# Moving two loads ahead of two transposing DMAs in a fused state-space and feed-forward kernel

## The chip, the cores and the metric

The kernel runs on one core of a Trainium2 chip. The metric is the device time of one execution in microseconds; the span of a profile (first to last instruction) is some 1.8 us shorter. Engines are named as in the profile: PE is TensorE, PEld its weight loads, DVE VectorE, ACT ScalarE, POOL GpSimd, SPq the queue on which SyncE issues DMAs. "L845" is a line of the kernel.

## The reference, cut to what matters

```python
xn  = layernorm(x)                                   # x: 2048 x 512, bf16
out = x + A(xn) + B(xn)
B   = (silu(xn @ w_gate) * (xn @ w_up)) @ w_down     # 512 -> 1376 -> 512
# A: a complex diagonal recurrence over the 2048 rows
#    u = B_bar xn;  h[t] = Lam_bar * h[t-1] + u[t];  y = 2 Re(C h) + xn * Dskip
```

## The kernel before

The 2048 rows are worked on in four chunks of 512. A chunk is loaded (`x_sb`), normalised (`xn_sb`), transposed by a DMA (`xnT`; chunk 2's is laid into `scrC`), multiplied with the gate and up weights and with B, scanned on VectorE, and projected down with `wd` and the C weights `W`, which are made from the transposed C matrices (`CT`, laid into `hss`).

Every operation is a task with its dependencies; a list scheduler then orders the tasks of ScalarE, VectorE and GpSimd by their estimated times. The orders of TensorE and of the DMA queue are those of the program. Two rules matter here. A transposing DMA waits for all DMAs before it, and DMAs after it wait for it:

```python
if xpose:
    after = after + tuple(dma_tasks)
    fn = lambda e, dst=dst, src=src: e.dma_start_transpose(out=dst, in_=src)
...
else:
    if xp_state[0] is not None:
        after = after + (xp_state[0],)
```

And `xn_sb` holds twelve 128-row tiles for sixteen, so chunk 3 is normalised into the place of chunk 0, after chunk 0's skip product (which needs `dsk`, the skip vector) and the sum that follows it (`resid_chunk`). The program, in the part concerned:

```python
xt_chunk_dma(1)          # transpose of chunk 1
loads_stage_b2()         # x of chunk 2, C matrices, skip vector, x of chunk 3
...
xt_chunk_dma(2)
dma("ld_wd0", wd[:, 0:FT - 1, :], ...)      # down weights, 1280 KB
dma("ld_wd1", wd[0:fsz[-1], FT - 1, :], ...)
...                      # gate, up of chunk 1; B of chunk 2
resid_chunk(0)
ln_chunk(3)
xt_chunk_dma(3)
ffn_left()               # leftover gate and up columns of all four chunks (L845, L855)
dc_chunk(0)              # first down projection (L966, L977, L980)
```

Of the kernel before, what the change touches and what calls it, by code (L numbers as in the profile page):

```python
# [249 lines left out]
def bass_parallel_sum__ssm_conv_s5__swiglu_ffn__prompt_kernel(  # L250
# [32 lines left out]
    with es:  # L283
        block = es.enter_context(nc.Block(no_gpsimd_drain=True))

        def sb(name, shape, dt):
            return es.enter_context(nc.sbuf_tensor(name, shape, dt))
# [7 lines left out]
        x_sb = sb("x_sb", [128, NT, D], B16)  # L295
# [14 lines left out]
        dsk = sb("dsk", [128, D], B16)  # L310
# [77 lines left out]
        x_v = A_x[0].rearrange("(a p) d -> p a d", p=128)  # L388
# [7 lines left out]
        def dma(name, dst, src, writes, nbytes, reads=(), after=(), out_=False, eng="sp", xpose=False, prio=0.0, order=(), **kw):  # L396
            after = tuple(after)
# [3 lines that stand above are left out]
                est, nb = 1900.0, int(nbytes * 1.2) + 140000  # L401
# [3 lines that stand above are left out]
                fn = lambda e, dst=dst, src=src: e.dma_start(dst, src, **kw)  # L405
                est, nb = 330.0 + nbytes / 900.0, nbytes
            t = g.add(eng, fn, reads=reads, writes=writes, name=name, dma=True, after=after, out=out_, est=est, nbytes=nb, prio=prio, order=order)
            dma_tasks.append(t)
            if xpose:
                xp_state[0] = t  # L410
            return t

        TILEB = 128 * D * 2
# [33 lines left out]

        def loads_stage_b2():
            dma("ld_x8", x_sb[:, 8:12, :], x_v[:, 8:12, :], [("x", a) for a in range(8, 12)], 4 * TILEB)
            dma("ld_cre", CT[:, 0], A_C_re, [("CT", 0)], 512 * 512 * 2, xpose=True)  # L450
            dma("ld_cim", CT[:, 1], A_C_im, [("CT", 1)], 512 * 512 * 2, xpose=True)
            dma("ld_dsk", dsk[:], A_Dskip.partition_broadcast(128), [("dsk",)], 128 * 1024)
            dma("ld_x12", x_sb[:, 12:16, :], x_v[:, 12:16, :], [("x", a) for a in range(12, 16)], 4 * TILEB)

        g.add("pool", lambda e: e.memset(epst[:], EPS), writes=[("epst",)], name="epst", est=100)
        g.add("pool", lambda e: e.memset(mhalf[:], -0.5), writes=[("mhalf",)], name="mhalf", est=100)
# [541 lines left out]
        loads_stage_b1()  # L998
        xt_chunk_dma(1)
        loads_stage_b2()  # L1000
        for ip in range(0, 3):
            ffn_up(0, ip)
# [97 lines left out]
```

## Time and profile before

| | before |
|---|---|
| time, median of 3 runs | 178.94 us (178.79 to 179.15) |
| the profiled execution | 179.2 us, span 177.4 us |
| TensorE, VectorE, ScalarE busy | 98%, 92%, 49% |
| TensorE waiting for data after 13.59 us | 0.33 us, at 64.52 |

The DMA queue in order of time shows the line of waits. Columns: start, time of the issue alone, queue and line, kind, destination and source.

```profile
42.16 0.34 SPq L405 DMA_DIRECT2D dsk<-in_A_Dskip_dram  x1
42.54 0.44 SPq L405 DMA_DIRECT2D x_sb<-in_A_x_dram  x1
47.35 1.69 SPq L400 DMA_TRANSPOSE scrC<-xn_sb  x1
51.62 1.14 SPq L405 DMA_DIRECT2D wd<-in_B_w_down_dram  x2
60.56 1.99 SPq L400 DMA_TRANSPOSE xnT<-xn_sb  x1
```

The short issue times are not the transfers; how long a transfer holds the queue is read from the distance to the next line. The skip vector and x of chunk 3 hold the queue from 42.16 to 47.35 us; the down weights hold it for 8.9 us, and only then does the transpose of chunk 3 go out. The rest of the profile before is read in the prediction.

### The profile page before, as it was taken

To read this page: it belongs to the slowest core of one execution; us is meant where nothing else is said; L and a number is where in the kernel's file an instruction comes from. 1 tells how busy PE (TensorE), PEld (TensorE's weight loads), DVE (VectorE), ACT (ScalarE), POOL (GpSimd) and SP (SyncE) were. 2 spreads that over 40 slices of the span, in tenths; PEclk is the share of its full clock that TensorE was granted. 3 is DMA by queue.
4 is the path that set the end of the run, shared out by engine and by line. 5 is a ranking of instruction groups with operands and counts; after the bars stand their busy time and mean duration, and the time that the engine had idled before them with its cause. 6 is when DMAs were issued, how large, how long until landed. Compare 5 with 4: busy or idle time off the path is not lost.

```text
span 177.4 us, 2425 instructions
## 1 busy us (share of the span) xinstructions
PE 173.9 (98%) x935; PEld 83.8 (47%) x935; DVE 162.5 (92%) x283; ACT 86.9 (49%) x116; POOL 11.1 (6%) x22
## 2 busy tenths in 40 slices
PE   8999999999999999999999999999999999999994
PEld 2894444444444434444444444444444444444644
DVE  2964999899899999999999999999999999999943
ACT  4679889979978869240456554000265520000000
POOL 3040500050050000000000000000000000000000
PEclk9999999999999999999999999999999999999999
DMA  5992595563468150001100000001100000000032
GB/s 169 268 373 68 120 148 95 161 133 82 134 133 283 29 102 0 0 4 66 54 0 0 0 0 4 0 0 59 59 0 4 0 0 0 0 0 30 32 110 67
DMA packets 22966, 12.37 MB, mean 70 GB/s; under 512 B 15180, under 2 KB 22956, under 8 KB 22956
## 3 DMA queue, kind: packets, MB, share of 16 engines
q1 hardware_dynamic: 22652, 11.77, 24.9%
q10 hardware_dynamic: 304, 0.46, 0.8%
q8 instruction: 7, 0.11, 0.3%
q14 instruction: 3, 0.02, 0.0%
HBM read 6.46 MB, written 2.10 MB: 48 GB/s over the span
## 4 chain that ended last, share of the span: by engine, by line
PE 62%; DMA 19%; DVE 7%; ACT 4%; SPq 3%; POOL 1%; issue 1%; ACTq 0%
PE pb L966 20%; PE pb L762 19%; PE pb L980 16%; DMA x_sb<-in_A_x_dram 7%; DMA xnT<-xn_sb 5%; PE pb L883 4%; SPq L405 3%; DVE st L483 3%; DMA hss<-in_A_C_im_dram 3%; DMA hss<-in_A_C_re_dram 2%; DMA dsk<-in_A_Dskip_dram 2%; PE pb L977 2%; ACT xn_sb L507 2%; DVE hT L834 1%; PE pb L855 1%
## 5 line engine op out<-in xcount | busy, mean ns | idle before, releaser
L923 DVE TENSOR_TENSOR_SCAN rot<-sm,car,rot 128x512 bf16<-128x512 f32 x32 | 38.8, 1266 | 0.0
L774 ACT ACTIVATE sg<-pb 128x1024 bf16<-128x1024 f32 x20 | 20.1, 1023 | 32.1 <-PE pb L762 31.3
L966 PE MATMUL pb<-wd,hT 128*128 128x512 bf16 (+2 forms) x180 | 35.2, 355 | 0.0
L980 PE MATMUL pb<-W,hss 128*128 128x512 bf16 (+2 forms) x144 | 30.3, 355 | 0.0
L762 PE MATMUL pb<-xnT,wu 128*128 128x512 bf16 x120 | 27.9, 379 | 0.0
L966 PEld LDWEIGHTS pb<-wd,hT 128*128 128x128 bf16 x180 | 16.8, 98 | 18.2 <-ACT scrC L730 0.4
L832 ACT ACTIVATE uf<-pb 128x1024 bf16<-128x1024 f32 x20 | 20.5, 1024 | 8.9 <-PE pb L762 7.3
L762 PE MATMUL pb<-xnT,wg 128*128 128x512 bf16 x92 | 21.8, 379 | 0.0
L883 PE MATMUL pb<-xnT,BT 128*128 128x512 bf16 x96 | 21.0, 379 | 0.0
L980 PEld LDWEIGHTS pb<-W,hss 128*128 128x128 bf16 x144 | 13.5, 97 | 14.4
L762 PEld LDWEIGHTS pb<-xnT,wu 128*128 128x128 bf16 x120 | 11.7, 98 | 14.2 <-ACT sg L774 0.2
L890 ACT ACTIVATE u_sb<-pb 128x1024 bf16<-128x1024 f32 x16 | 16.0, 1022 | 3.3 <-PE pb L883 3.3
L883 PEld LDWEIGHTS pb<-xnT,BT 128*128 128x128 bf16 x96 | 9.3, 98 | 11.4 <-DMA BT<-in_A_B_im_dram 0.3
L985 DVE TENSOR_TENSOR x_sb<-pb,x_sb 128x512 bf16<-128x512 f32 (+2 forms) x18 | 11.1, 628 | 3.3 <-PE pb L980 3.0
L762 PEld LDWEIGHTS pb<-xnT,wg 128*128 128x128 bf16 x92 | 9.0, 98 | 10.6
L834 DVE TENSOR_TENSOR hT<-sg,uf 128x1024 bf16<-128x1024 bf16 x20 | 13.4, 681 | 0.4 <-ACT uf L832 0.4
L483 DVE BATCH_NORM_STATS2 st<-x_sb 128x6 f32<-128x512 bf16 x12 | 7.4, 679 | 3.1 <-DMA x_sb<-in_A_x_dram 3.1
L914 DVE TENSOR_TENSOR rot<-u_sb,cosT 128x2048 bf16<-128x2048 bf16 x8 | 9.7, 1218 | 0.0
L914 DVE TENSOR_TENSOR rot<-rot,sin 128x2048 bf16<-128x2048 bf16 x8 | 9.7, 1218 | 0.0
L914 DVE TENSOR_TENSOR rot<-u_sb,sin 128x2048 bf16<-128x2048 bf16 x8 | 9.7, 1218 | 0.0
L914 DVE TENSOR_TENSOR rot<-rot,cosT 128x2048 bf16<-128x2048 bf16 x8 | 9.7, 1213 | 0.0
L914 DVE TENSOR_TENSOR rot<-rot 128x2048 bf16<-128x2048 bf16 x8 | 9.6, 1218 | 0.0
(93 smaller groups left out, 180.4 us busy)
## 6 DMA issues: line engine op xcount, KB each, us to landing
out_dram<-x_sb SPq DMA_DIRECT2D x15, 128.0 KB, 1.7
x_sb<-in_A_x_dram SPq DMA_DIRECT2D x3, 512.0 KB, 4.7
wd<-in_B_w_down_dram SPq DMA_DIRECT2D x1, 1280.0 KB, 8.6
wu<-in_B_w_up_dram SPq DMA_DIRECT2D x1, 768.0 KB, 5.0
wu<-in_B_w_up_dram SPq DMA_DIRECT2D x1, 608.0 KB, 7.0
x_sb<-in_A_x_dram SPq DMA_DIRECT2D x4, 128.0 KB, 3.2
wg<-in_B_w_gate_dram SPq DMA_DIRECT2D x1, 480.0 KB, 5.9
wg<-in_B_w_gate_dram ACTq DMA_DIRECT2D x1, 448.0 KB, 3.8
```

Source lines behind the costliest of these rows:

```text
L483: return g.add("dve", lambda e, a=a: e.bn_stats(out=st[:, a % 8, :], in_=x_sb[:, a, :]), reads=[("x", a)], writes=[("st", a % 8), ("st0", ...
L762: inst = e.matmul(pbank[0:fs, bk, :].rearrange("p (j t) -> p j t", j=4), lhsT=w[:, kt, i * 128:i * 128 + fs], rhs=xnT[c][:, :, kt, :], sta ...
L774: g.add("act", lambda e: e.activation(out=sg[rows, sl, 0:n, :].rearrange("p a t -> p (a t)"), in_=pair_f32(rows, bk, 512 * n), func=AF.Sil ...
L832: g.add("act", lambda e: e.activation(out=uf[rows, ul, 0:n, :].rearrange("p a t -> p (a t)"), in_=pair_f32(rows, bk, 512 * n), func=AF.Ide ...
L834: g.add("dve", lambda e: e.tensor_tensor(out=hT[rows, hb, i0:i0 + n, :], in0=sg[rows, sl, 0:n, :], in1=uf[rows, ul, 0:n, :], op=ALU.mult), ...
L883: inst = e.matmul(pbank[:, bk, :].rearrange("p (j t) -> p j t", j=4), lhsT=BT[:, ri, kt, pt * 128:(pt + 1) * 128], rhs=xnT[c][:, :, kt, :] ...
L890: g.add("act", lambda e: e.activation(out=u_sb[:, us].rearrange("p r t -> p (r t)"), in_=pair_f32(slice(0, 128), b0), func=AF.Identity), r ...
L914: tt = lambda out, a, b, op, r, w, nm: g.add("dve", lambda e: e.tensor_tensor(out=out, in0=a, in1=b, op=op), reads=r, writes=w, name="%s_% ...
L923: g.add("dve", lambda e, A0=A0, A1=A1, k=k, ri=ri, pt=pt: e.tensor_tensor_scan(out=A1[:, k, ri, :], data0=rr[:, pt:pt + 1].to_broadcast([1 ...
L966: inst = e.matmul(pbank[:, bk, 0:nc_], lhsT=hT[0:fs, hb, i, lt * 128:(lt + 1) * 128], rhs=wd[0:fs, i, c0:c0 + nc_], start=(i == 0), stop=F ...
L980: inst = e.matmul(pbank[:, bk, 0:nc_], lhsT=hss[:, hb, pt, ri, lt * 128:(lt + 1) * 128], rhs=W12[:, ri, pt, c0:c0 + nc_], start=False, sto ...
L985: g.add("dve", lambda e, bk=bk, a=a, c0=c0, nc_=nc_: e.tensor_tensor(out=x_sb[:, a, c0:c0 + nc_], in0=pbank[:, bk, 0:nc_], in1=x_sb[:, a, ...
```

## The change

Its intent: have chunk 3 in the core and the skip vector at hand some ten microseconds sooner, so that the scheduler can normalise chunk 3 on ScalarE between the evacuations of chunk 1 (an evacuation is the instruction that copies a finished product out of `pb`, TensorE's output buffer). The arguments are cut here:

```diff
         def loads_stage_b2():
             dma("ld_x8", x_sb[:, 8:12, :], ...)
+            dma("ld_x12", x_sb[:, 12:16, :], ...)
+            dma("ld_dsk", dsk[:], A_Dskip.partition_broadcast(128), ...)
             dma("ld_cre", CT[:, 0], A_C_re, [("CT", 0)], 512 * 512 * 2, xpose=True)
             dma("ld_cim", CT[:, 1], A_C_im, [("CT", 1)], 512 * 512 * 2, xpose=True)
-            dma("ld_dsk", dsk[:], A_Dskip.partition_broadcast(128), ...)
-            dma("ld_x12", x_sb[:, 12:16, :], ...)
```

More of the change, by code (lines that the diff above doesn't have):

```diff
@@ L449, in loads_stage_b2 @@
             dma("ld_x8", x_sb[:, 8:12, :], x_v[:, 8:12, :], [("x", a) for a in range(8, 12)], 4 * TILEB)
+            dma("ld_x12", x_sb[:, 12:16, :], x_v[:, 12:16, :], [("x", a) for a in range(12, 16)], 4 * TILEB)
+            dma("ld_dsk", dsk[:], A_Dskip.partition_broadcast(128), [("dsk",)], 128 * 1024)
             dma("ld_cre", CT[:, 0], A_C_re, [("CT", 0)], 512 * 512 * 2, xpose=True)
             dma("ld_cim", CT[:, 1], A_C_im, [("CT", 1)], 512 * 512 * 2, xpose=True)
-            dma("ld_dsk", dsk[:], A_Dskip.partition_broadcast(128), [("dsk",)], 128 * 1024)
-            dma("ld_x12", x_sb[:, 12:16, :], x_v[:, 12:16, :], [("x", a) for a in range(12, 16)], 4 * TILEB)
         g.add("pool", lambda e: e.memset(epst[:], EPS), writes=[("epst",)], name="epst", est=100)
```

## The prediction

> **What bounds the kernel now.** I read the page first, for the busy shares; then the chain of work that ended last, to see from where on one engine alone sets the end; then TensorE in order of time, to measure how much of its time is a gap that a change could close; then the DMA queue's own waits, for what makes that gap. The page's busy line:
>
> ```profile
> PE 173.9 (98%) x935; PEld 83.8 (47%) x935; DVE 162.5 (92%) x283; ACT 86.9 (49%) x116; POOL 11.1 (6%) x22
> ```
>
> TensorE is shown busy 98% of the span of 177.4 us. A busy share can hide loosely spaced matmuls, so I checked the spacing. From 84.10 to 101.36 us the trace has 80 matmuls of 512 columns: 17.26 / 80 = 0.2158 us from start to start. With that spacing I walked through TensorE in order of time. From 13.59 to 37.76 us stand 112 matmuls (112 x 0.2158 = 24.17 us, and 24.17 are shown), from 37.76 to 61.93 another 112 (again 24.17), from 67.67 to 76.31 the 40 of the first down projection (8.63; 8.64 are shown), and from there to 173 us each group starts when its predecessor's count is spent. Only this place is loose:
>
> ```profile
> 61.93 1.89 PE L845 MATMUL pb<-xnT,wg 128*128 128x512 bf16 x8
> 63.66 1.03 PE L845 MATMUL pb<-scrC,wg 128*128 128x512 bf16 x4
> 64.85 1.04 PE L845 MATMUL pb<-xnT,wg 128*128 128x512 bf16 x4 [0.17 <-DMA xnT<-xn_sb]
> 65.82 1.05 PE L855 MATMUL pb<-xnT,wu 128*64 128x512 bf16 x8
> ```
>
> These are the leftover feed-forward columns of all four chunks (a chunk is 512 rows of x). The four matmuls from 63.66 are spent at 63.66 + 4 x 0.2158 = 64.52; the next, the first that read chunk 3, start at 64.85. The bracket shows 0.17 us idle because a matmul's modelled end is late; by the spacing the loss is **0.33 us**. Two more losses, 0.11 us before 65.82 and 0.12 us within the 64-row tiles that follow, are marked "issue": they belong to the change of tile form, not to a wait. So some 0.33 us of the kernel between 13.59 and 173 us is a wait for data, and all of it is for the transposed chunk 3. The chain of waits tells where that came from:
>
> ```profile
> 29.81 3.43 DMA x_sb<-in_A_x_dram
> ...
> 33.26 4.16 DMA hss<-in_A_C_re_dram
> ...
> 37.43 4.71 DMA hss<-in_A_C_im_dram
> ...
> 42.16 3.76 DMA dsk<-in_A_Dskip_dram
> ...
> 54.09 2.93 ACT xn_sb L507 x4
> ...
> 60.56 4.25 DMA xnT<-xn_sb
> 64.81 0.05 issue
> 64.85 1.04 PE pb L845 x4
> ```
>
> Two things are to be seen. The loads stand in one line: the kernel makes each transposing DMA wait for all DMAs before it and each later DMA wait for the transpose. And after 64.85 us the chain is TensorE alone until the last add. But the chain's account of 54 to 60 us is too simple: ScalarE had normalised chunk 3 by 57.02 us, yet its transpose was issued at 60.56. The DMA queue's own waits have the real last releaser, the load of the down weights, issued from 51.62 to 52.76 and waited for until 60.46:
>
> ```profile
> SPq L244 <- DMA wd<-in_B_w_down_dram: 7.7, 1, 7.7
> ```
>
> **What the Trainium skill says.** "Perfetto Trace Analysis", section "Identifying the Most-Contended Engine", holds matmul busy share for a poor measure because matmuls are pipelined; this trace agrees, which is why I used the spacing (a record is 0.379 us long where the spacing is 0.2158). "DMA: Bandwidth & Descriptors", section "Issuing engines are not separate DMA queues", says that transfers share the same 16 DMA engines and interleave, and section "Latency and other measured facts" puts most of a DMA's fixed cost at about 2 us. The trace agrees: stores of 128 KB take 1.7 us to land, and the 512 KB load alone 3.43 us, so four times the bytes cost twice the time. Loads issued together should therefore share one fixed cost.
>
> **The change part by part.** No instruction is added or removed; two loads move ahead of the two C transposes, and the list scheduler inside the kernel then orders ScalarE and VectorE anew. TensorE's and the DMA queue's orders are the program's, so TensorE keeps its order wholly.
>
> 1. Loads. The x load of chunk 2 is still issued at 29.81 us. The x load of chunk 3 and the skip vector follow without a wait. From stores to loads the slope is (3.43 - 1.7) / 384 KB = 0.0045 us per KB; 640 KB more make 3.43 + 2.9 = 6.3 us, so all three land near 36.2 us (estimate). Chunk 3 of x then lands about 11 us before its present 47.3, the skip vector about 10 before its 45.9.
> 2. C transposes. The first is issued at 36.2 instead of 33.26, the second lands at 36.2 + 4.16 + 4.71 = 45.1 instead of 42.14: **3 us later**.
> 3. The transpose of chunk 2 no longer waits for the x load of chunk 3: 45.1 instead of 47.35, **2.2 us earlier**. TensorE wants it at 55.02 us, now as before with time to spare.
> 4. The down weights follow it 4.3 us later: issued at 49.4 rather than 51.62, and with the same 8.8 us (51.62 to 60.46) landed at 58.2.
> 5. The transpose of chunk 3: issued at 58.3 if the normalisation is done, landed at 58.3 + 4.25 = 62.5. TensorE wants it at 64.52, so the wait of 0.33 us goes, with 2.0 us to spare.
> 6. Normalisation. Statistics on VectorE (4 x 0.68 and 4 x 0.15 us), 2.4 us on GpSimd, the skip product and sum of chunk 0 that free the buffer (2 x 1.2 us), and four activations of 0.73 us on ScalarE can start near 36 us rather than 47. ScalarE is full from 40 to 50 us (10.0 of 10), so they will lie between evacuations, and the eight scalings of the C matrices move to where the normalisation was, at 54 us. All of this is beside TensorE.
>
> The sum on the path: 0.33 us less, of 178.94. That is 0.2%.
>
> **The rivals.** *The C weights become late.* They come 3 us later and are needed when TensorE begins the second half of the first down projection:
>
> ```profile
> 73.01 0.75 DVE L737 SCALAR_TENSOR_TENSOR W<-hss,sm,scrC 128x512 bf16<-128x512 bf16 x1
> 73.68 0.68 DVE L872 TENSOR_TENSOR hL<-sg,uf 96x1024 bf16<-96x1024 bf16 x1
> ```
>
> VectorE ends them at 73.75 and TensorE reads them from 76.53, a margin of 2.8 us (the leftover product, done at 74.36 and read at 76.31, has 2.0). Against the rival: ScalarE's first scaling of C runs at 44.59 us, only half a microsecond ahead of the new landing, and VectorE reaches the first product only at 66.11 us. VectorE has no less and no more to do by then, and loses a wait of 0.74 us for the skip vector. If it struck, 0.5 to 2 us would be lost.
>
> *ScalarE becomes late.* Four activations, 2.9 us, put ahead of evacuations would hold PSUM banks. At 41.88 us ScalarE is already 2.4 us behind TensorE; a bank pair comes round after four groups of 1.73 us. The gate group that ended at 39.5 must be evacuated by 44.66 and is so at 42.8: 1.9 us of margin, less than the 2.9 if all four went there. But the present order normalises chunk 2 there without a stall, and the scheduler weighs a task by the work behind it, which is longer for these evacuations. Cost if it struck: about 1 us.
>
> *VectorE becomes the bound.* It is busy 92%, and the last state product, from 163.40 to 165.76 us, is read by TensorE from 167.28: a margin of 1.5 us. A late x of chunk 2 (it now shares the DMA engines) would idle VectorE by up to 2 us near 33 us; half would be met by the waits that vanish. Loss 0 to 1 us.
>
> *It is hidden anyway.* The earlier x could gain nothing because the down weights, not the normalisation, release the last transpose. But those weights move up too (step 4), so I hold the gap closed.
>
> **Range and chances.** Point: 178.94 - 0.33 = 178.6 us. Above it, the three rivals, each with a chance of about one in ten of about 1 us; below, little, for no second gap exists. The three runs before spread by 0.36 us. I give 178.1 to 179.4. A gain of 2% (3.6 us) would need matmuls to go away: 0.01. A loss of 2% would need a rival at several times its margin: 0.03.
>
> **What would show it.** Right: the four matmuls on chunk 3 start 0.87 us after the four before them, with no wait; the queue issues the second x load within a microsecond of the first; the transpose of chunk 2 is issued near 45 and that of chunk 3 near 58 us; the normalisation of chunk 3 stands among chunk 1's evacuations; the span shrinks by about 0.3 us. Wrong: a new TensorE gap in 40 to 62 us released by ScalarE (evacuations), at 76 us by VectorE (C weights), or near 167 us by VectorE (last state product).

## The result, and the profile after

| | before | after |
|---|---|---|
| time, median of 6 runs | 178.80 us (178.65 to 179.15) | 178.88 us (178.70 to 179.27) |
| ratio of the means | | 1.0004, 95% interval 0.9991 to 1.0018 |
| the profiled execution | 179.2 us, span 177.4 | 178.82 us, span 177.1 |

Ratios here are the mean time of one kernel's fast runs over that of the other's fast runs of the same rounds, so not quite the ratio of the medians in the table.

The time is inside the predicted range, but the gain of 0.33 us would be a ratio of 0.9982, and that is outside the measured interval, which ends at 0.9991. Yet the two profiles, side by side, show exactly that gain. The DMA queue of the changed kernel:

```profile
29.66 0.93 SPq L405 DMA_DIRECT2D x_sb<-in_A_x_dram  x2
30.64 0.50 SPq L405 DMA_DIRECT2D dsk<-in_A_Dskip_dram  x1
35.57 1.97 SPq L400 DMA_TRANSPOSE hss<-in_A_C_re_dram  x1
...
44.01 1.77 SPq L400 DMA_TRANSPOSE scrC<-xn_sb  x1
48.26 1.10 SPq L405 DMA_DIRECT2D wd<-in_B_w_down_dram  x2
54.93 2.03 SPq L400 DMA_TRANSPOSE xnT<-xn_sb  x1
```

The transpose of chunk 2 goes out at 44.01 instead of 47.35 us, that of chunk 3 at 54.93 instead of 60.56. TensorE in order of time, changed kernel:

```profile
63.65 1.03 PE L845 MATMUL pb<-scrC,wg 128*128 128x512 bf16 x4
64.51 1.03 PE L845 MATMUL pb<-xnT,wg 128*128 128x512 bf16 x4
65.47 1.05 PE L855 MATMUL pb<-xnT,wu 128*64 128x512 bf16 x8
```

The distance over the place of the gap is now 0.86 us (before, from 63.66 to 64.85: 1.19) and no wait is marked. The chain that ended last is TensorE from its first matmul on:

```profile
PE 98%; DVE 0%; issue 0%
```

ScalarE in order of time has the four normalisations of chunk 3 where the change wanted them, one after each of four evacuations of chunk 1 in a row. The first two:

```profile
43.87 1.02 ACT L774 ACTIVATE sg<-pb 128x1024 bf16<-128x1024 f32 x1
44.77 0.82 ACT L507 ACTIVATE xn_sb<-x_sb,nmr,rstd 128x512 bf16<-128x512 bf16 x1
45.48 1.02 ACT L832 ACTIVATE uf<-pb 128x1024 bf16<-128x1024 f32 x1
46.38 0.82 ACT L507 ACTIVATE xn_sb<-x_sb,nmr,rstd 128x512 bf16<-128x512 bf16 x1
```

And VectorE ends the C weights at 72.35 + 0.76 = 73.11 us, before TensorE reads them at 76.18:

```profile
72.35 0.76 DVE L737 SCALAR_TENSOR_TENSOR W<-hss,sm,scrC 128x512 bf16<-128x512 bf16 x1
```

So two profiles differ by 0.34 us at the place foretold, and the timed runs do not differ. Both cannot be typical.

### The profile page after: what moved, and what is told of

It reads as the page before. It is cut to its first block, busy times and chain, and to the rows that moved or that the text cites. A ratio compares the mean times of both kernels' runs of the same rounds, so it can differ in the third digit from the quotient of the medians.

```text
span 177.1 us, 2424 instructions
## 1 busy us (share of the span) xinstructions
PE 173.8 (98%) x935; PEld 84.0 (47%) x935; DVE 162.8 (92%) x283; ACT 87.3 (49%) x116; POOL 10.9 (6%) x22
## 4 chain that ended last, share of the span: by engine, by line
PE 98%; DVE 0%; issue 0%
PE pb L762 36%; PE pb L966 20%; PE pb L980 16%; PE pb L883 16%; PE pb L806 4%; PE pb L478 3%; PE pb L977 2%; PE pb L845 2%; PE pb L855 1%; PE pb L585 1%; DVE x_sb L985 0%
```

## The experiments

**Theory A**: the wait of 0.33 us is not in most executions of the kernel before; the first profile caught a run in which the down weights landed late, and what the change gives is slack ahead of the last transpose, not time. **Rival B**: the wait is in every run, and the change gives the time back at another place. **Rival C**: the gain is real and the timing missed it. Twelve runs were made, all with correct results.

### The two kernels once more, unchanged

No edit. First the kernel before, timed against itself:

> The unchanged kernel once more, timed against itself and profiled again. Theory A (the wait of 0.33 us on the transposed chunk 3 that the first profile showed is not in most executions: that profile was of a run of 179.2 us, where the median is 178.8, and its load of the down weights took 8.8 us where the profile of the changed kernel has 6.7): the load of the down weights takes 6 to 7.5 us, the transpose of chunk 3 is issued before 59.5 us, and the four matmuls on chunk 3 start 0.86 us after the four before them, with no wait; time ratio 1.000. Rival B (the wait is in every run, and the change gives its 0.33 us back elsewhere): the load takes 8 to 9 us and the gap of 0.33 us is there again.

Ratio 0.9996, interval 0.9963 to 1.0028. Its profiled execution (205.4 us, granted clock 0.853 instead of 1.0) is not used for the wait; its load of the down weights is used once below. The changed kernel in the same rounds:

> The changed kernel once more, for a second profile and a narrower interval. Theory A: ratio 0.999 to 1.001, no TensorE gap, transpose of chunk 3 landed near 59.5 us, 5 us before it is wanted. Rival B: the same ratio, but the profile shows somewhere else a new TensorE gap of about 0.3 us. Rival C (a real gain that the first timing missed): ratio 0.998.

Median 178.76 us, ratio 0.9982, interval 0.9956 to 1.0007. This sits on rival C's number, but the interval holds 1.000 as well, and the narrower first one does not reach down to 0.9982. The two intervals overlap from 0.9991 to 1.0007; timing alone does not decide between no gain and a small one. Its profile has no TensorE gap anywhere after 13.9 us, which speaks against B. Then four more looks at the kernel before:

> The unchanged kernel, a third profile. Theory A: down weights in 6 to 7.5 us and no gap before the matmuls on chunk 3. Rival B: 8 to 9 us and a gap of 0.33 us.

> The unchanged kernel, a fourth profile. Theory A: as the third, no gap. Rival B: a gap of 0.33 us. A mixture of the two over the four profiles would say that the load's time varies from run to run.

> The unchanged kernel, for the share of runs with a wait before the matmuls on chunk 3. Theory A: the down weights take 7 to 9 us, and the tail behind the bulk of them is as long as the one instruction fetch (16 KB) that lies in the load, about 1.2 us where it is ordinary; a gap only if both the fetch is long and the start early. So no gap here, with 0.3 to 1.5 us to spare.

> The unchanged kernel once more. Theory A: as the one before it, no gap, or one under 0.4 us with a fetch of over 2 us in the load of the down weights.

All four ran at a granted clock of 1.00 (178.92, 179.39, 178.67 and 178.70 us), as the fast runs do, and **none has the gap**. The first two ran on one chip and the last two on another; the chip of the first profile is not on record, but its execution is one of the six of the first timing, which found no difference. In the first of them, the second profile of before, TensorE shows

```profile
63.76 1.03 PE L845 MATMUL pb<-scrC,wg 128*128 128x512 bf16 x4
64.62 1.03 PE L845 MATMUL pb<-xnT,wg 128*128 128x512 bf16 x4
```

with 0.86 us from line to line, as in the changed kernel. The table has, for every profile at full clock, when the down weights and the transpose of chunk 3 were issued, and the margin. "Wanted" is when TensorE could start on chunk 3: the start of the four matmuls before, and 4 x 0.2158 = 0.863 us for them. The margin is that less the landing, which is taken as the issue and 4.25 us, the time that the chain of the first profile shows (so it is an estimate for the others).

| profile | down weights issued | transpose of chunk 3 issued | wanted | margin, us |
|---|---|---|---|---|
| before, the first | 51.62 | 60.56 | 64.52 | -0.29 |
| before, 2nd | 51.86 | 59.10 | 64.62 | 1.3 |
| before, 3rd | 52.16 | 60.24 | 65.08 | 0.6 |
| before, 4th | 51.03 | 58.70 | 64.36 | 1.4 |
| before, 5th | 51.37 | 59.04 | 64.40 | 1.1 |
| after, the first | 48.26 | 54.93 | 64.51 | 5.3 |
| after, 2nd | 47.13 | 53.71 | 64.83 | 6.9 |

From issue to issue the load of the down weights took 8.9 us in the first profile and 7.2 to 8.1 in the others; with the change 6.7 and 6.6. The second and third profiles had been expected at 6 to 7.5 us and have 7.2 and 8.1. The bytes moved over 52 to 61 us, in forty slices of 0.225 us, show what is long in it. The first profile before, the second before, and the first after:

```profile
GB/s 0 0 18 137 137 369 223 155 255 255 364 364 346 373 369 337 350 355 369 369 378 301 155 68 36 23 27 23 23 27 23 23 27 23 23 14 0 0 0 0
```

```profile
GB/s 0 0 0 18 146 50 264 205 137 250 287 328 360 391 373 387 396 373 369 382 382 355 355 291 114 46 23 23 27 5 0 0 0 0 0 0 18 203 218 209
```

```profile
GB/s 369 360 314 369 387 391 360 232 187 23 5 0 0 0 0 0 0 0 117 222 216 213 206 223 212 220 215 206 212 70 0 0 0 0 0 0 0 0 0 0
```

The bulk runs at 350 to 390 GB/s; then comes a tail at 23 GB/s, a sixteenth of that, which is what one of the 16 DMA engines finishing alone would give. It lasts some 2.7 us in the first profile, 1.1 in the second and 0.4 in the changed kernel. In the first profile the only instruction fetch in that stretch (16 KB) took 2.6 us of one engine; in the other profiles of before it took 1.0 to 1.4 us:

```profile
q8 instruction: 1, 0.02, 1.8%
```

(1.8% of 16 engines over 9 us is 2.6 us.) That the longest fetch and the longest tail fall together suggests a cause; but the fifth profile, with a fetch of 1.0 us, still took 7.7 us for the load, so the length of the fetch is not all of it.

Where the fetch falls says more. In the six profiles with the old order in which the load was long (7.0 to 8.6 us to land: the five of the table and the reload run below), the fetch began 1.2 to 2.8 us after the load was issued. In the seven with one or both loads moved, it began 5.5 to 5.8 us after, when the load was nearly done, and the load landed in 6.1 to 6.6 us. The slow profile of the unchanged kernel is the one with the old order and no fetch inside the load (it began 8.9 us after the issue): its load landed in 6.4 us, with no long tail. So the change also brings the load ahead of the fetch, and part of its slack goes with that: 0.5 to 1.5 us, by 7.2 to 8.1 us from issue to issue in the ordinary runs before against 6.6 and 6.7. All 14 profiles agree, but no run moves the fetch alone, so that the fetch makes the tail is not shown.

What follows: theory A. One of five full-clock profiles of the kernel before has the wait, none of the two of the changed one. Were that its share, the mean gain would be 0.33 / 5 = 0.07 us, or 0.04%, below what these rounds resolve. Other waits swing as much: the profile of the run of 179.39 us (the third of before) lost time at B's second matrix, where nothing was changed:

```profile
25.36 6.86 PE L883 MATMUL pb<-xnT,BT 128*128 128x512 bf16 x31 [0.30 <-DMA BT<-in_A_B_im_dram]
```

The four matmuls ahead of it started at 24.03, so the next could have started at 24.89: 0.47 us were lost. And the second profile of the changed kernel, 179.16 us, waited 0.47 us for the first gate weights before 6.05 us. So a long run does not by itself tell which wait it had.

### How much slack there is: the down weights loaded a second time

If the change bought slack, a delay put ahead of the last transpose must cost the kernel before nearly all of itself, and the changed one nothing up to its margin. Half of the down weights are copied once more, after the first copy and before the transpose. The task is put in after scheduling, so no compute engine changes its order. Applied to the kernel before, then to the changed one (shortened):

```diff
         streams = _schedule(g.tasks, engs)
+        again = g.add("sp", lambda e: e.dma_start(wd[:, 0:5, :], B_w_down[0:5 * 128, :]...), dma=True, after=(ld_wd0, ld_wd1))
+        streams["sp"].insert(streams["sp"].index(xTd3), again)
+        xTd3.deps.add(again)                # and the down projections wait for it
```

> The kernel before with half of the down weights (640 KB) loaded a second time, right before the transpose of chunk 3; the orders of all compute engines are kept. The copy waits for the first load, so it delays that transpose by 3.5 to 4.5 us. Theory A (before, the transposed chunk 3 lands only 0 to 1.3 us ahead of TensorE's need): a TensorE gap of 2.5 to 4 us ahead of the matmuls on chunk 3, and the time 2.5 to 4 us longer, 181.4 to 183. Rival (the transpose has several microseconds of slack in most runs): under 1 us longer.

> The changed kernel with the same second load of 640 KB before the transpose of chunk 3, compute orders kept. Theory A (the change bought 4 to 5 us of slack there and nothing else): the transpose lands near 63.5 us, still ahead of TensorE's need at 64.5, and the time stays within 0.3 us of 178.8. Rival: it becomes 2 to 4 us longer, as in the kernel before.

The kernel before became 184.72 us (ratio 1.0303, interval 1.0283 to 1.0323); the changed kernel stayed at 179.18 (ratio 0.9997, interval 0.9982 to 1.0012; before was 179.23 in these rounds). **The same delay costs 5.5 us in one and nothing that the timing can show in the other.** The changed kernel's TensorE passes the place without a wait, its transpose issued at 59.46:

```profile
63.90 1.03 PE L845 MATMUL pb<-scrC,wg 128*128 128x512 bf16 x4
64.77 1.03 PE L845 MATMUL pb<-xnT,wg 128*128 128x512 bf16 x4
```

The second copy held the queue from 60.28 to 64.41 us (4.1 us) in the kernel before and from 55.20 to 59.46 (4.3 us) in the changed one. The 5.5 us are more than the 2.5 to 4 expected. TensorE in the delayed kernel before:

```profile
64.07 1.03 PE L845 MATMUL pb<-scrC,wg 128*128 128x512 bf16 x4
68.78 1.04 PE L845 MATMUL pb<-xnT,wg 128*128 128x512 bf16 x4 [3.69 <-DMA xnT<-xn_sb]
```

The gap is 68.78 - 64.07 - 0.86 = 3.85 us, as expected. The rest is the clock. The stretches after it, with busy time of PE, PEld, DVE, ACT and POOL, then granted clock, DMA share and GB/s:

```profile
64.90:68.80 3.90, 0.21 (x2) 0.02 (x2) 3.90 (x5) 2.13 (x3) 0.00 (x0) 1.00 0.71 134
68.80:71.00 2.20, 2.20 (x12) 0.91 (x14) 2.20 (x4) 0.00 (x0) 0.00 (x0) 0.76 0.00 0
71.00:73.20 2.20, 2.20 (x13) 0.67 (x10) 2.07 (x3) 1.57 (x3) 0.00 (x0) 0.50 0.00 0
73.20:76.00 2.80, 2.80 (x15) 1.27 (x14) 2.80 (x5) 2.47 (x4) 0.00 (x0) 0.97 0.00 0
```

The granted clock fell to 0.50 soon after the idle stretch: the mean of 0.76 from 68.80 to 71.00 puts the fall near 70 us (an estimate), some 5 us after the last matmul before the gap, and by 73.3 us it was back. From the first matmul on chunk 3 to the down projection it took 73.17 - 68.78 = 4.39 us, where the second profile of before has 67.43 - 64.62 = 2.81: another 1.6 us. Gap and clock make 5.4 of the 5.5 us. The Trainium skill, "TensorE: Matmul & The Clock Gate", section "What's actually happening", says that the gate falls to half after an idle window of about 3.4 us; this run agrees (3.85 us idle, clock 0.50), and the wait of 0.33 us in the first profile, with its clock at 1.00, is far from it.

The changed kernel with all ten blocks copied again (`0:10`):

> The changed kernel with all ten blocks of the down weights (1280 KB) loaded a second time there: a delay of 5.5 to 7 us against a slack of 5. Theory A: a TensorE gap of 0.5 to 2 us and the time as much longer, 179.3 to 180.8. Rival (slack much larger than 5 us): no gap.

Expected was a loss of 0.5 to 2 us; measured 179.35 us, ratio 1.0009 (0.9985 to 1.0033). The transpose went out at 60.32 and TensorE waited 0.10 us (64.65, where 63.69 + 0.86 = 64.55 was possible). A miss in size: the margin was taken as 5 us from one profile, and the second of the changed kernel has 6.9. The extra load, from 54.16 to 60.32, fitted almost wholly. It puts the slack of the changed kernel near 6 us in this run, against 0.6 to 1.4 in the ordinary runs before.

### Which part of the change gives the slack

Only the loads, with ScalarE and VectorE kept in the order of the kernel before:

```diff
         streams = _schedule(g.tasks, engs)       # the tasks as before
+        # then move ld_x12 and ld_dsk right behind ld_x8 in the DMA queue,
+        # let them wait for the transpose of chunk 1 only, and the C transposes for them
```

> Only the order of the loads is changed, as in the changed kernel; ScalarE and VectorE keep the order of the kernel before, so chunk 3 is still normalised in one block late in chunk 1. Theory A (the earlier normalisation on ScalarE is worth nothing, the load order is all): chunk 3 normalised by 57 to 58 us, its transpose issued then and landed near 62, no TensorE gap, time 178.5 to 179.1. Rival (ScalarE's new order matters): a gap before the matmuls on chunk 3 or at the C weights, and a longer time by 0.3 us or more.

178.89 us, ratio 0.9989 (0.9973 to 1.0006), no gap. ScalarE normalises chunk 3 in one block, later than in the changed kernel, and the transpose leaves when it is done:

```profile
53.07 2.93 ACT L507 ACTIVATE xn_sb<-x_sb,nmr,rstd 128x512 bf16<-128x512 bf16 x4 [0.33 <-DVE nmr L504]
```

It was issued at 56.02, about a microsecond after the changed kernel's 54.93, and landed an estimated 4.2 us ahead of TensorE. So the earlier normalisation, the change's stated aim, is worth some 1 to 3 us of slack (the changed kernel's 5.3 and 6.9 against 4.2) and no time; the load order gives the other 3 or so (4.2 against 0.6 to 1.4).

Then each load alone moved ahead, with the scheduler free:

> Half of the change: only the x load of chunk 3 is moved ahead of the C transposes; the skip vector still follows them. Theory A (each load left between the last C transpose and the transpose of chunk 2 costs that path a whole transfer of about 4 us, so the slack needs both moved): the skip vector lands near 47.5 us, the transpose of chunk 2 is issued there, as before the change, the down weights land near 59 to 60.5 and the transpose of chunk 3 is issued 0 to 1.5 us ahead of the latest good time. Rival (the slack comes mostly from the 512 KB of x): the transpose of chunk 2 is issued by 45.5 and that of chunk 3 by 57.

> The other half: only the skip vector is moved ahead of the C transposes. Theory A: the x load of chunk 3 still stands before the transpose of chunk 2, which is issued near 46.5 to 47.5 us; that of chunk 3 at 59 to 60.5. Rival: the skip vector, slow to land, was what held the pair, and the transpose of chunk 2 is issued by 45.5.

| moved ahead | transpose of chunk 2 issued | of chunk 3 issued | margin, us |
|---|---|---|---|
| nothing (second profile) | 47.60 | 59.10 | 1.3 |
| x of chunk 3 | 45.93 | 56.71 | 3.3 |
| skip vector | 45.69 | 56.37 | 3.8 |
| both (first profile) | 44.01 | 54.93 | 5.3 |

Theory A's detail fell here: the load left behind does not cost the path as much as the pair. Alone the skip vector held the queue from 42.99 to 45.93 (2.9 us) and x of chunk 3 from 42.36 to 45.69 (3.3 us), the two together from 42.16 to 47.35 in the first profile (5.2 us). Either half gives about half of the slack, also against the fourth and fifth profiles of before, which ran on the same chip as these two (transpose of chunk 2 issued at 46.77 and 47.09, margins 1.4 and 1.1). Of that, 0.8 to 1.4 us come from the earlier transpose of chunk 2, and much of the rest from the shorter load of the down weights, 6.5 and 6.4 us from issue to issue. Single runs took 178.59 and 178.68 us; with one run each no difference in time is claimed.

No run points to a version that beats both kernels by this route: with the wait gone, in the first profile of the changed kernel, TensorE keeps its spacing from 13.57 us to the end, but for the 0.2 us at the change of tile form, and an earlier load can only add slack.

## Why the prediction was right or wrong, point by point

- **What bounds the kernel**: right. The chain of the changed kernel is TensorE from end to end, and the medians stay at 178.8 to 178.9 us.
- **Loads together near 36.2 us**: they had landed by 35.57. Right, as was that the x load of chunk 2 would hardly suffer: VectorE began its statistics at 33.11 instead of 33.26.
- **C transposes 3 us later**: the first was issued 2.3 us later, and the next transpose, which waits for the second one, went out at 44.01 rather than 45.1.
- **Transpose of chunk 2 2.2 us earlier**: 3.3 us.
- **Down weights landed at 58.2**: about 54.9. The step took 8.8 us for the load from the one profile; it took 6.7, and 6.6 in the second profile of the changed kernel. That the load would be shorter, as it is in every profile in which the instruction fetch comes only near its end, the prediction did not foresee.
- **Transpose of chunk 3 issued at 58.3, 2.0 us to spare**: 54.93, and about 5 to spare; the extra lead comes from the two steps before and was not foreseen.
- **Normalisation between evacuations, nothing late**: right. No rival struck: no wait for an evacuation shows in TensorE's spacing, and the C weights were 3.1 us ahead of need (76.18 - 73.11). Of the eight scalings of the C matrices only the four early ones moved, to between 51.21 and 56.93 us; the prediction had all eight move.
- **"The sum on the path: 0.33 us less"**: the failed term. Its mechanism was right, and in the first profile of the changed kernel the wait is gone; its size was not. It took the 0.33 us of one execution for a cost of every execution, though that execution was the slowest of the three timed runs listed beside it (179.15). Four further full-clock profiles have none of it, with 0.6 to 1.4 us of margin, and the first timing puts the ratio at 1.0004, not 0.9982. The point of 178.6 us was 0.3 us too low; the range, drawn wide for the rivals, held the 178.88. That the time lies inside is owed to that width, not to the sum.
- **"It is hidden anyway"**, the rival that was set aside, is what happened, for another reason than the one weighed there: in the ordinary run the old order was already in time.

## What to carry to other kernels

Before counting a small wait as gain, compare the profiled execution's time with the timed runs and take a second and third profile: a wait that is near the run-to-run spread may belong to one run. The time alone does not tell: the changed kernel's profile of 179.16 us has no such wait. A transfer that lands before it is wanted yields slack and no time, and a deliberate delay put in its way measured that slack here where timing could not: the same 640 KB cost 5.5 us without it and nothing measurable with it. Where transposing DMAs are kept in one line with all others, as here, each load moved out from between two of them let what stood behind it start earlier.

## What the Trainium skill lacked or had wrong

- "Perfetto Trace Analysis", section "Identifying Performance Opportunities", tells how to find the gaps on the bounding engine, but not that a gap can be of one execution: here one full-clock profile of five had it, 0.33 us, in a run of 179.2 us against a median of 178.8.
- "DMA: Bandwidth & Descriptors" gives bandwidths by size, but no spread from run to run and no figure for a load beside an instruction fetch: the same load of 1376 KB held the queue for 6.6 to 8.9 us in the seven full-clock profiles of the two kernels, with a tail at 23 GB/s, a sixteenth of the bulk's rate, of 0.4 to 2.7 us in the three shown. The long tails stand where a fetch began early in the load; that it makes them is not shown.
